# Gathering sampled V rows by two indirect transfers of GpSimd instead of six addressed ones of SP

## The chip, the cores and the metric

The kernel runs on one core of a Trainium2 chip. The metric is the device time of one execution in microseconds; the time before is the median of three runs, 924.11 us (923.51 to 927.22). Times below are us from the start of the profiled execution's span unless ns is said. The engines are PE (TensorE), DVE (VectorE), ACT (ScalarE), POOL (GpSimd) and SP (SyncE), which here only issues transfers.

## The reference

Block-sparse attention over 4 batches, 8 heads, 768 positions and head size 64, followed by a feed-forward layer. Positions are in 24 blocks of 32. A query block sees its neighbours, the first and the last block, and three sampled blocks; the first and last query blocks see all.

```python
mask = np.abs(blk_i - blk_j) <= window
mask = mask | (blk_i == 0) | (blk_j == 0) | (blk_i == n_blocks - 1) | (blk_j == n_blocks - 1)
for qb in range(n_blocks):
    for kb in sampled_blocks[qb]:
        mask[qb*block:(qb+1)*block, kb*block:(kb+1)*block] = True
scores = np.where(mask, scale * q @ k.T, -1e9)
attn = softmax(scores)
x = (attn @ v)            # heads side by side: 3072 tokens x 512
h = x @ w_in              # 512 x 2048
out = np.maximum(0.01 * h, h) @ w_out
```

The sampled block numbers are an input, so which rows are read is known only when the kernel runs.

## The kernel before, in words

Two query blocks of a batch make a tile T (12 a batch; tile 0 holds the first and last block and sees all keys). The other 11 tiles, 44 in all, each get their 12 visible blocks copied together: slots 0 to 3 are the neighbourhood, 4 and 5 the first and last block, 6 to 11 the sampled blocks of the two query blocks. 12 slots of 32 are 384 keys, three chunks of 128.

- `gather_k` fills `kg` from `kt` (K turned, in SBUF): slots 0 to 5 by DVE, the six sampled ones by POOL, as two tasks of three copies (line 1005). Each task first reads three offsets from the small table `offs` into registers (line 982, TENSOR_LOAD).
- `gather_v` fills `vg` from `scr`, a table in DRAM with one row of 2 KB for each position (8 heads, each value split into a high and a low half of 16 bits). Slots 0 to 3 come by one SP transfer of 128 rows, slots 4 and 5 by two SP transfers once a batch and buffer. The six sampled slots are two tasks of SP: a load of three offsets (line 982), then three transfers of 32 rows whose address is a register (line 1036). `vg` has two buffers, so a tile's V can be fetched when PE's products with the tile two before are done.
- A unit is one head pair of a tile. PE makes the scores `s` from `kg` and the turned queries `qs` and `qxs` (heads swapped); DVE adds the mask and takes the maximum (`p`, `mx`); ACT takes the exponential; `pp` is the normalised probability in two halves (ACT the high, DVE the low one); an SP transfer turns it into `pt` (DMA_TRANSPOSE; in the first quarter of the first batch PE does it); PE forms `av` from `pt` and `vg`. ACT and DVE take `av` out as `xf`, and ACT and POOL split it into `x`.
- Four tiles make an item of 256 tokens, whose feed-forward runs beside the attention of later items: PE makes `h` from `x` and the weights `W`, ACT and DVE make `ht`, DVE the high half of `g` and POOL its low half, PE `o`; ACT scales it into `ob` and SP stores it.
- At the start `load_constants` and `build_masks` read the sampled block numbers and build `offs` and the mask; the weights arrive and are decoded until about 250 us.

All of this is recorded as tasks (line 384 is the helper that records most of them), and a planner then sets the order on every engine: it plays the tasks forward with costs from `cost` and `CFG`, each engine taking the ready task of the lowest priority number, and writes down the order. The chip then keeps that order on each engine, with semaphores for what depends on other engines. So a cost in `CFG` or in `cost` is no work; it changes the order. In the order listings `waits PE` means PE's semaphore, `DMAHW` and `DMASW` the counter of an earlier transfer issued by SP or POOL.

Of the kernel before, what the change touches and what calls it, by code (L numbers as in the profile page):

```python
# [16 lines left out]
I32 = mybir.dt.int32  # L17
AF = mybir.ActivationFunctionType
ALU = mybir.AluOpType
AX = mybir.AxisListType  # L20

P = 128
BLOCK = 32
# [5 lines left out]
SLOTS = 12  # L29
# [3 lines left out]
    "ahead": 3,  # L33
    "av_lag": 3,
    "bs": 1500,
    "early": 2,
    "flag": 1,
    "g": 2,
    "g_at": 0,
# [348 lines left out]
def cost(eng, method, a, k):  # L388

    out = k.get("out", a[0] if a else None)  # L390
    n = elements(out)
    apply = lambda x: hasattr(x, "ap")
    if eng == "PE":
        lhs, rhs = a[1], a[2]
        cols = elements(rhs)
        if lhs.dtype == F32:
            return 60.0 + 4 * cols, 300.0 + 4 * cols, "f", []
        half = elements(lhs) <= 64
        t = (cols / 2.4 + 2.5) / CFG["clock"]
        return (t / 2 if half else t), t + 180, ("a" if half else "f"), []  # L400
    if eng == "SP" or method.startswith("dma"):
        turned = method == "dma_start_transpose"
        w = transfer(k["out"], k["in_"], turned)
        rows = len([d for d in list(k["out"].ap) if d[1] > 1])
        busy = 1050.0 + 0.37 * n if turned else 380.0 + 110 * max(0, rows - 1)
        return busy, busy, "", [w]
    if eng == "DVE":
        ptr = sum(1 for x in (k.get("scalar"), k.get("scalar1"), k.get("scale")) if apply(x)) > 0
        src = [x for m, x in k.items() if m in ("in0", "in1", "in_") and apply(x)]
        wide = [x for x in src if elements(x) > 1]  # L410
        f = 1.0
        if method in ("tensor_copy", "tensor_scalar") and len(wide) == 1 and wide[0].space == bass.MemoryType.SB:
            f = 0.5
            if method == "tensor_copy" and wide[0].dtype == F16 and out.dtype == F16:
                f = 0.25
        if method == "tensor_reduce":
            n = elements(k["in_"])
        d = 145 + 62 * ptr + n * f / 0.96
        if len(wide) == 2 and all(x.space == bass.MemoryType.SB for x in wide) and n >= 256:
            d *= 1.08  # L420
        acc = method == "tensor_tensor_reduce"
        return max(d - 70, 60.0), d + 12 + 80 * acc, "", []
    if eng == "ACT":
        src = a[1]
        ptr = any(apply(k.get(x)) for x in ("scale", "bias"))
        d = n * 0.833 + (155 if src.space == bass.MemoryType.PSUM else 187) + 93 * ptr
        acc = "accum_out" in k
        return d - 92 + 100 * acc, d + 14 + 93 * acc, "", []
    d = 120 + n * (2.2 if method == "tensor_tensor" else 1.3)
    return d + 20, d + 12, "", []  # L430
# [3 lines left out]
def tile_block_sparse_attention_ffn(  # L434
# [165 lines left out]
    iota = cst.tile([NB, NB], F32, name="iota")  # L600
    tmps = pf.tile([P, DM], F32, tag="ob", name="tmps", bufs=CFG["ob"])
    sb = tmps[:NB, :2 * NR].bitcast(I32)
    row = tmps[:1, 6:6 + 2 * NB * NR].bitcast(I32)
    eq = tmps[:NB, 150:150 + NR * NB].rearrange("p (r b) -> p r b", r=NR)
    sels = [tmps[:NB, 222 + P * a:222 + P * (a + 1)].rearrange("p (a b c) -> p a b c", a=2, b=2) for a in range(2)]
    assert 222 + 2 * P <= DM and 6 + 2 * NB * NR <= 150
    offs = cst.tile([1, NT - 1, 2, 4], I32, name="offs")
    mask = cst.tile([P, NT - 1, SLOTS], F32, name="mask")

    def load_constants():  # L610
        nc.sync.dma_start(out=eye, in_=c_eye)
        nc.vector.tensor_copy(out=eye16, in_=eye)
        nc.sync.dma_start(out=row, in_=sampled.bitcast(I32).rearrange("(o a) b -> o (a b)", o=1))
        nc.sync.dma_start(out=allow, in_=c_allow)
        nc.sync.dma_start(out=iota, in_=c_iota)
        nc.sync.dma_start(out=sb, in_=sampled.bitcast(I32))

    def build_masks():
        blocks = row.rearrange("p (a b) -> p a b", b=2)[:, NR:NR + (NT - 1) * 2 * NR, 0]
        nc.vector.memset(offs, 0)  # L620
        nc.vector.tensor_scalar(
            out=offs[:, :, :, :NR], in0=blocks.rearrange("p (t a r) -> p t a r", a=2, r=NR), scalar1=0, scalar2=NB - 1,
            op0=ALU.max, op1=ALU.min)
        nc.vector.tensor_scalar(out=offs, in0=offs, scalar1=5, scalar2=None, op0=ALU.logical_shift_left)
        sf = cst.tile([NB, NR], F32, name="sf")
        nc.vector.tensor_copy(out=sf, in_=sb.rearrange("p (a b) -> p a b", b=2)[:, :, 0])

        ok = cst.tile([NB, NR], F32, name="ok")
        hit = cst.tile([NB, NB], F32, name="hit")
        for r in range(NR):  # L630
            nc.vector.tensor_scalar(out=eq[:, r, :], in0=iota, scalar1=sf[:, r:r + 1], scalar2=None, op0=ALU.is_equal)
            nc.vector.tensor_tensor(out=hit, in0=eq[:, r, :], in1=allow, op=ALU.mult)
            nc.vector.tensor_reduce(out=ok[:, r:r + 1], in_=hit, op=ALU.add, axis=AX.X)
            nc.vector.tensor_tensor(out=allow, in0=allow, in1=eq[:, r, :], op=ALU.max)
        nc.vector.tensor_scalar(out=ok, in0=ok, scalar1=-1.0, scalar2=1.0, op0=ALU.mult, op1=ALU.add)

        at = cst.tile([NB, NT - 1, 2, NR], F32, name="at")
        nc.gpsimd.affine_select(
            out=at.rearrange("p t a r -> p (t a) r"), in_=ok.unsqueeze(1).to_broadcast([NB, NB - 2, NR]),
            pattern=[[-1, NB - 2], [0, NR]], base=-1, channel_multiplier=1,  # L640
            compare_op=ALU.is_equal, fill=0.0)
        pm = corner()[:, :(NT - 1) * 2 * NR].rearrange("p (t a r) -> p t a r", t=NT - 1, a=2)
        for a in range(2):
            sel = sels[a]
            nc.vector.memset(sel, 0.0)
            nc.vector.memset(sel[:, :, a, :], 1.0)
            nc.tensor.matmul(
                pm[:, :, a, :], sel.rearrange("p a b c -> p (a b c)"), at[:, :, a, :], start=True, stop=True)
        nc.vector.tensor_scalar(
            out=mask[:, :, 6:], in0=pm.rearrange("p t a r -> p t (a r)"), scalar1=-1.0, scalar2=-NEG,  # L650
            op0=ALU.add, op1=ALU.mult)
        nc.vector.memset(mask[:, :, :6], 0.0)
        for hh in range(2):
            a, b = (slice(D * hh + BLOCK * i, D * hh + BLOCK * (i + 1)) for i in range(2))
            nc.vector.memset(mask[a, :, 3:4], NEG)
            nc.vector.memset(mask[b, :, 0:1], NEG)
            nc.vector.memset(mask[a, 0:1, 4:5], NEG)
            nc.vector.memset(mask[b, NT - 2:NT - 1, 5:6], NEG)
# [318 lines left out]
    kgs, vgs = {}, {}  # L977
    last_use = {}

    def sampled_of(T, a, engine):  # L980

        _, rows = tc.nc.values_load_multi_w_load_instructions(
            offs.ap[:1, T - 1, a, :NR], engines={engine}, min_val=0, max_val=S - BLOCK,
            skip_runtime_bounds_check_because="the block numbers are clamped to the sequence before they are shifted")
        return zip(range(6 + a * NR, 6 + (a + 1) * NR), rows)

    kgb = [pa.tile([P, H, KEYS], F16, tag=f"kg{i}", name=f"kg{i}", bufs=1) for i in range(2)]
    ends = {}
# [1 line left out]
    def gather_k(b, T):  # L990
# [6 lines left out]
        if ends.get(n) != b:  # L997
            ends[n] = b
            nc.vector.tensor_copy(
                out=kg[:, :, P:P + Q2].rearrange("p h (n l) -> p h n l", l=BLOCK),  # L1000
                in_=kt.rearrange("p h (n l) -> p h n l", l=BLOCK)[:, :, 0:NB:NB - 1, :])
        for a in range(2):
            def copies(a=a):
                for slot, off in sampled_of(T, a, mybir.EngineType.Pool):
                    tc.nc.gpsimd.tensor_copy(  # L1005
                        out=kg.ap[:, :, slot * BLOCK:(slot + 1) * BLOCK], in_=kt.ap[:, :, bass.ds(off, BLOCK)])
            at = (6 + a * NR) * BLOCK
            plan.task("POOL", copies, 2150.0, 2150.0, cells(kt) | cells(offs), cells(kg[:, :, at:at + NR * BLOCK]))
            yield
        em = pa.tile([P, KEYS], BF16, tag="em", name=f"em_{b}_{T}", bufs=2)  # L1010
        nc.gpsimd.tensor_copy(
# [8 lines left out]
    def gather_v(b, T):  # L1020
# [6 lines left out]
        if vends.get(n) != b:  # L1027
            vends[n] = b
            for slot, a in ((4, 0), (5, S - BLOCK)):
                ps, c = place(slot)  # L1030
                nc.sync.dma_start(out=vg[ps, c, :], in_=scr[b][a:a + BLOCK, :])
        for a in range(2):
            def moves(a=a):
                for slot, off in sampled_of(T, a, mybir.EngineType.SP):
                    ps, c = place(slot)
                    tc.nc.sync.dma_start(out=vg.ap[ps, c, :], in_=scr[b].ap[bass.ds(off, BLOCK), :])
            into = set()
            for slot in range(6 + a * NR, 6 + (a + 1) * NR):
                ps, c = place(slot)
                into |= cells(vg[ps, c, :])  # L1040
            plan.task("SP", moves, 1850.0, 1850.0, cells(scr[b]) | cells(offs), into, "",
                      [BLOCK * (9.3 + 0.055 * 2048) / 16] * NR)
        vgs[b, T] = vg.rearrange("p c (h x) -> p c h x", h=H)


# [577 lines left out]
```

## Time and profile before

| | |
|---|---|
| Median of the runs | 924.11 us (923.51 to 927.22) |
| Profiled execution | 927.57 us, of it 925.9 us span |
| Busy over the span | PE 83%, DVE 68%, ACT 55%, POOL 36% |
| Transfers issued by SP, all by its hardware queue | 65.7% of the 16 transfer engines' span |
| Sampled V transfers | 264 (44 tiles of six), 88 loads of offsets on SP |
| Sampled K copies | 264 on POOL, 515 ns each in the mean, 88 loads of offsets |

The page gives busy time of each engine and the costliest groups of instructions: count, busy time, mean ns, idle time before them and what ended it. A view by stage gives busy time between two times. The view of waits says which instruction stood idle and which engine or transfer ended that. Of SP the timeline and the view by line show when it issues and how long an issue takes (least, median, most, in ns); SP's issuing does not count as busy time.

### The profile page before, as it was taken

The numbers are of one execution on the slowest core, as the hardware profiler recorded it, in microseconds if no ns is written. First come the engines' busy times: TensorE is split into PE (matmuls) and PEld (weight loads), VectorE is DVE, ScalarE is ACT, GpSimd is POOL, SyncE is SP. The second block draws the span as 40 slices with busy tenths as digits, with TensorE's granted clock in tenths as the row PEclk, the third lists the DMA queues.
The fourth block names the chain that finished last, engine by engine and source line by source line (L and its number), as shares of the span: only waits on it lengthen the run. The fifth ranks groups of instructions, "written<-read, shape, count | busy, mean of one in ns | idle before, by whom it ended". The sixth has DMA issues, their size and how long they took to land. (4 is left out here: it accounts for less than half of the span.)

```text
span 925.9 us, 20826 instructions
## 1 busy us (share of the span) xinstructions
PE 767.3 (83%) x7204; PEld 499.0 (54%) x7204; DVE 626.3 (68%) x1650; ACT 509.4 (55%) x1087; POOL 330.0 (36%) x469
## 2 busy tenths in 40 slices
PE   2647566688889978988788988988898899999998
PEld 2425443444556645555554655655565555656664
DVE  4698789998979945856748657667467466474221
ACT  5678766556655635645546556556357355274121
POOL 0234356523324523433413433324314344242221
PEclk9566678888999999999999999999999999999999
DMA  9504896488797767798677878786765867466000
GB/s 182 201 18 124 256 237 171 115 197 166 149 169 168 169 133 153 155 175 160 138 169 132 169 148 161 177 155 138 166 146 123 161 125 156 89 133 125 1 23 24
DMA packets 312231, 133.29 MB, mean 144 GB/s; under 512 B 275005, under 2 KB 287294, under 8 KB 312126
## 3 DMA queue, kind: packets, MB, share of 16 engines
q1 hardware_dynamic: 312126, 131.96, 65.7%
q8 instruction: 57, 0.93, 0.4%
q14 instruction: 48, 0.39, 0.1%
HBM read 65.57 MB, written 12.58 MB: 84 GB/s over the span
## 5 line engine op out<-in xcount | busy, mean ns | idle before, releaser
L384 PEld LDWEIGHTS <-W 128*128 128x128 f16 (+1 forms) x2480 | 237.8, 101 | 83.6 <-DVE W L384 24.5
L384 PE MATMUL o<-W,g 128*128 128x512 f16 x1152 | 278.1, 388 | 4.0 <-DVE g L384 2.8
L384 PE MATMUL h<-x,W 128*128 128x256 f16 x2304 | 278.4, 276 | 3.0 <-ACT x L384 2.1
L384 POOL TENSOR_TENSOR g<-ht,g 128x512 f16<-128x512 f32 x96 | 117.1, 1220 | 285.0 <-DVE g L384 207.0
L384 PEld LDWEIGHTS <-g 128*128 128x128 f16 x1152 | 109.6, 100 | 132.5 <-issue 21.0
L384 DVE SCALAR_TENSOR_TENSOR pp<-p,r,pp 128x384 f16<-128x384 f32 x208 | 147.6, 738 | 45.6 <-ACT pp L384 45.1
L384 ACT ACTIVATE p<-p,mx 128x384 f32<-128x384 f32 x208 | 125.8, 606 | 91.9 <-DVE mx L384 91.2
L1005 POOL COPY kg<-kt 128x256 f16 x264 | 125.9, 515 | 138.5 <-PE s L384 113.7
L384 ACT ACTIVATE pp<-p,r 128x384 f16<-128x384 f32 x208 | 118.8, 606 | 75.4 <-DMA pt<-pp 26.8
L384 PE MATMUL av<-pt,vg 128*64 128x128 f16 x2112 | 90.5, 228 | 54.5 <-DMA vg<-scr 29.6
L384 DVE SCALAR_TENSOR_TENSOR ht<-h,gd,ht 128x512 f32<-128x512 f32 x80 | 59.9, 749 | 106.3 <-ACT ht L384 105.8
L384 DVE CUSTOM_DVE_ANT_0 p<-s,em,nsc 128x384 f32<-128x384 f32 x176 | 104.7, 609 | 31.6 <-PE s L384 30.6
L384 ACT ACTIVATE ht<-h,gs 128x512 f32<-128x512 f32 x80 | 54.5, 681 | 118.4 <-PE h L384 110.7
L384 PEld LDWEIGHTS <-vg 128*64 128x64 f16 x2112 | 71.8, 114 | 88.4 <-issue 70.2
L384 PE MATMUL s<-kg,qs 128*64 128x384 f16 x352 | 64.0, 354 | 15.9 <-DVE mx L384 14.0
L384 POOL TENSOR_TENSOR x<-xf,x 128x256 f16<-128x256 f32 x48 | 35.9, 747 | 96.2 <-ACT x L384 96.0
L384 PE MATMUL s<-kg,qxs 128*64 128x384 f16 x352 | 63.5, 349 | 4.7 <-DMA qxs<-qs 4.7
L384 PEld LDWEIGHTS <-qs 128*64 128x64 f16 x416 | 29.2, 114 | 40.9 <-issue 32.0
L384 DVE CAST g<-ht 128x512 f16<-128x512 f32 x96 | 42.5, 443 | 10.8 <-PE o L384 6.5
L384 ACT ACTIVATION_READ_ACCUMULATOR p<-p,mx 128x1 f32 x208 | 39.1, 188 | 0.0
L384 DVE TENSOR_SCALAR sum<-sum 128x2 f32<-128x2 f32 x96 | 28.5, 297 | 15.3 <-ACT p L384 14.7
L384 POOL TENSOR_TENSOR W<-W 128x1024 f16<-128x1024 f32 x12 | 28.1, 2349 | 27.9 <-ACT W L384 25.6
(117 smaller groups left out, 759.8 us busy)
## 6 DMA issues: line engine op xcount, KB each, us to landing
vg<-scr SPq DMA_DIRECT2D x280, 64.0 KB, 1.9
vg<-scr SPq DMA_DIRECT2D x44, 256.0 KB, 3.2
v<-in_v_dram SPq DMA_DIRECT2D x32, 192.0 KB, 4.2
qxs<-qs SPq DMA_DIRECT2D x48, 128.0 KB, 2.4
scr<-v SPq DMA_DIRECT2D x16, 384.0 KB, 3.3
rq<-in_q_dram SPq DMA_DIRECT2D x20, 256.0 KB, 3.9
W<-in_moe_w_in_dram SPq DMA_DIRECT2D x5, 1024.0 KB, 7.5
out_dram<-ob SPq DMA_DIRECT2D x20, 256.0 KB, 2.5
```

The lines of the kernel that those rows point to most:

```text
L384: self.plan.task(self.eng, lambda: f(*a, **k), busy, late, reads, writes, kind, loads)
L1005: tc.nc.gpsimd.tensor_copy(out=kg.ap[:, :, slot * BLOCK:(slot + 1) * BLOCK], in_=kt.ap[:, :, bass.ds(off, BLOCK)])
```

## The change

The six sampled transfers of SP and their two loads of offsets go. In their place POOL issues two indirect transfers a tile, which take the row numbers from a table in SBUF, `vrow`, one number for each partition: one fills partitions 64 to 127 of chunk 1 (slots 6 and 7), one the whole of chunk 2 (slots 8 to 11). They come from the same rows of `scr`. `vrow` is built at the start: the block numbers are now copied to all 128 partitions (`rows`), clamped, shifted by 5, and the lane within the block is added (`lane`, by POOL's iota). K's two loads of three offsets become one load of six, whose registers the second task of copies uses too. The planner gets costs for the new tasks, and other costs for an SP transfer (425 instead of 380 ns) and K's copies.

```diff
-    "early": 2,
+    "kcopy": 560.0, "load": 800.0, "fetch": 1100.0, "early": 2,
...
-        busy = 1050.0 + 0.37 * n if turned else 380.0 + 110 * max(0, rows - 1)
+        busy = 1050.0 + 0.37 * n if turned else 425.0 + 110 * max(0, rows - 1)
...
-        nc.sync.dma_start(out=row, in_=sampled.bitcast(I32).rearrange("(o a) b -> o (a b)", o=1))
+        nc.sync.dma_start(
+            out=rows, in_=sampled.bitcast(I32).rearrange("(o a) b -> o (a b)", o=1).to_broadcast([P, 2 * NB * NR]))
...
+        nc.gpsimd.iota(lane.rearrange("p a t -> p (a t)"), pattern=[[0, 2 * (NT - 1)]], base=0, channel_multiplier=1)
+        nc.vector.tensor_scalar(out=lane, in0=lane, scalar1=BLOCK - 1, scalar2=None, op0=ALU.bitwise_and)
+        nc.vector.memset(vrow, 0)
+        for n in range(2 * NR):
+            at, c = (n if n < 2 else n - 2) * BLOCK, int(n >= 2)
+            nc.vector.tensor_scalar(
+                out=vrow[at:at + BLOCK, c, :], in0=of_tile[at:at + BLOCK, :, n], scalar1=0, scalar2=NB - 1,
+                op0=ALU.max, op1=ALU.min)
+        nc.vector.tensor_scalar(out=vrow, in0=vrow, scalar1=5, scalar2=None, op0=ALU.logical_shift_left)
+        nc.vector.tensor_tensor(out=vrow, in0=vrow, in1=lane, op=ALU.add)
...
             def copies(a=a):
-                for slot, off in sampled_of(T, a, mybir.EngineType.Pool):
+                if not a:
+                    found.extend(sampled_of(T, mybir.EngineType.Pool))
+                for slot, off in found[a * NR:(a + 1) * NR]:
...
-        for a in range(2):
-            def moves(a=a):
-                for slot, off in sampled_of(T, a, mybir.EngineType.SP):
-                    ps, c = place(slot)
-                    tc.nc.sync.dma_start(out=vg.ap[ps, c, :], in_=scr[b].ap[bass.ds(off, BLOCK), :])
...
+        for c, n0 in ((1, P - 2 * BLOCK), (2, 0)):
+            at = vrow[:P - n0, c - 1, T - 1:T]
+            into = vg[n0:, c, :]
+
+            def fetch(at=at, into=into):
+                tc.nc.gpsimd.indirect_dma_start(
+                    into.ap, None, scr[b].ap, bass.IndirectOffsetOnAxis(ap=at.ap, axis=0))
+            plan.task("POOL", fetch, CFG["fetch"], CFG["fetch"], cells(scr[b]) | cells(at), cells(into), "",
+                      [(P - n0) * (9.3 + 0.055 * 2048) / 16])
```

The order on SP in the second batch, where its V for one tile is fetched while the next batch's V comes in (`vg0` is the first V buffer, `scr1` the table, `pt4` and `pt5` turned probabilities), before:

```order
L384 DMA_TRANSPOSE pt4_154<-pp0_137 128x6x128 [waits DMAHW0_49,DVE_49,PE_49]
L384 DMA vg0_86<-scr1_72 128x1024 [waits DMAHW1_49,PE_49]
L982 TENSOR_LOAD offs_80
L1036 ISA
L1036 DMA vg0_86<-scr1_72 32x1024 [waits DMAHW2_49,PE_49]
L1036 ISA
L1036 DMA vg0_86<-scr1_72 32x1024 [waits DMAHW3_49]
L1036 ISA
L1036 DMA vg0_86<-scr1_72 32x1024 [waits DMAHW4_49,PE_49]
L384 DMA_TRANSPOSE pt5_155<-pp1_138 128x6x128 [waits DMAHW5_49,DVE_49]
L982 TENSOR_LOAD offs_80
```

And now, at the same tile:

```order
L384 DMA_TRANSPOSE pt2_151<-pp2_144 128x6x128 [waits DMAHW0_49,DVE_49,PE_49]
L384 DMA_TRANSPOSE pt3_152<-pp3_145 128x6x128 [waits DMAHW1_49,DVE_49,PE_49]
L384 DMA v3_110<-in_v_dram 128x6x64 [waits DMAHW2_49]
L384 DMA v3_110<-in_v_dram 128x6x64 [waits DMAHW3_49]
L384 DMA vg0_88<-scr1_72 128x1024 [waits DMAHW4_49,PE_49]
L384 DMA v4_137<-in_v_dram 128x6x64 [waits DMAHW5_49]
L384 DMA v4_137<-in_v_dram 128x6x64 [waits DMAHW6_49]
L384 DMA_TRANSPOSE pt4_156<-pp0_139 128x6x128 [waits DMAHW7_49,DVE_49]
L384 DMA_TRANSPOSE pt5_157<-pp1_140 128x6x128 [waits DMAHW0_49,DVE_49,PE_49]
```

Between the transposes SP has only plain transfers left; the two loads and six moves of the tile are gone.

POOL in the same batch, where one tile's K is copied and the feed-forward goes on (`kg` the K buffers, `g` and `x` the low halves that PE's o and h read), before:

```order
L384 TENSOR_TENSOR g_210<-ht,g_210 128x512 [waits DVE_49]
L982 TENSOR_LOAD offs
L1005 ISA
L1005 COPY kg_85<-kt_83 128x8x32 [waits PE_49]
L1005 ISA
L1005 COPY kg_85<-kt_83 128x8x32
L1005 ISA
L1005 COPY kg_85<-kt_83 128x8x32
L384 TENSOR_TENSOR x_215<-xf,x_215 128x4x64 [waits Activation_49]
L982 TENSOR_LOAD offs
```

And now:

```order
L1055 DMA vg_88<-scr_72,vrow 64x1024 [waits DMASW4_49,PE_49]
L384 TENSOR_TENSOR g_216<-ht,g_216 128x512 [waits DVE_49,Pool_49]
L384 TENSOR_TENSOR x_217<-xf,x_217 128x4x64 [waits Activation_49]
L1055 DMA vg_88<-scr_72,vrow 128x1024 [waits DMASW5_49,PE_49]
L995 TENSOR_LOAD offs
L1021 ISA
L1021 COPY kg_86<-kt_85 128x8x32 [waits PE_49,Pool_49]
```

A fetch that waits for PE now stands ahead of g and x, and another ahead of the next tile's K copies.

DVE in the first 20 us, ahead of the first turned K (`kt`), now (before, the row of `vrow` is not there and the others follow each other in the same way):

```order
L384 CAST eye_76<-eye 128x128
L384 TENSOR_SCALAR vrow<-ob_79 32x11 x5
L384 COPY kt_97<-h_68 128x768
L384 COPY kt_97<-h_67 128x768
L384 TENSOR_SCALAR totk_147<-s_64 128x1
```

Five of the rows that build `vrow` (from the table of block numbers, which lies in an `ob` buffer) stand ahead of K's copies.

More of the change, by code (lines that the diff above doesn't have):

```diff
@@ L602, in tile_block_sparse_attention_ffn @@
     sb = tmps[:NB, :2 * NR].bitcast(I32)
-    row = tmps[:1, 6:6 + 2 * NB * NR].bitcast(I32)
+    rows = tmps[:, 6:6 + 2 * NB * NR].bitcast(I32)
     eq = tmps[:NB, 150:150 + NR * NB].rearrange("p (r b) -> p r b", r=NR)
@@ L606, in tile_block_sparse_attention_ffn @@
     assert 222 + 2 * P <= DM and 6 + 2 * NB * NR <= 150
-    offs = cst.tile([1, NT - 1, 2, 4], I32, name="offs")
+    offs = cst.tile([1, NT - 1, 8], I32, name="offs")
+    vrow = cst.tile([P, 2, NT - 1], I32, name="vrow")
+    lane = cst.tile([P, 2, NT - 1], I32, name="lane")
     mask = cst.tile([P, NT - 1, SLOTS], F32, name="mask")
@@ L618, in build_masks @@
     def build_masks():
-        blocks = row.rearrange("p (a b) -> p a b", b=2)[:, NR:NR + (NT - 1) * 2 * NR, 0]
+        of_tile = rows.rearrange("p (a b) -> p a b", b=2)[:, NR:NR + (NT - 1) * 2 * NR, 0].rearrange(
+            "p (t a) -> p t a", a=2 * NR)
         nc.vector.memset(offs, 0)
         nc.vector.tensor_scalar(
-            out=offs[:, :, :, :NR], in0=blocks.rearrange("p (t a r) -> p t a r", a=2, r=NR), scalar1=0, scalar2=NB - 1,
-            op0=ALU.max, op1=ALU.min)
+            out=offs[:, :, :2 * NR], in0=of_tile[:1], scalar1=0, scalar2=NB - 1, op0=ALU.max, op1=ALU.min)
         nc.vector.tensor_scalar(out=offs, in0=offs, scalar1=5, scalar2=None, op0=ALU.logical_shift_left)
+        nc.gpsimd.iota(lane.rearrange("p a t -> p (a t)"), pattern=[[0, 2 * (NT - 1)]], base=0, channel_multiplier=1)
[8 more added lines that the diff above has]
+        nc.vector.tensor_tensor(out=vrow, in0=vrow, in1=lane, op=ALU.add)
         sf = cst.tile([NB, NR], F32, name="sf")
@@ L978, in tile_block_sparse_attention_ffn, with sampled_of @@
     last_use = {}
-    def sampled_of(T, a, engine):
+    def sampled_of(T, engine):
         _, rows = tc.nc.values_load_multi_w_load_instructions(
-            offs.ap[:1, T - 1, a, :NR], engines={engine}, min_val=0, max_val=S - BLOCK,
+            offs.ap[:1, T - 1, :2 * NR], engines={engine}, min_val=0, max_val=S - BLOCK,
             skip_runtime_bounds_check_because="the block numbers are clamped to the sequence before they are shifted")
-        return zip(range(6 + a * NR, 6 + (a + 1) * NR), rows)
+        return list(zip(range(6, SLOTS), rows))
     kgb = [pa.tile([P, H, KEYS], F16, tag=f"kg{i}", name=f"kg{i}", bufs=1) for i in range(2)]
@@ L1001, in gather_k @@
                 in_=kt.rearrange("p h (n l) -> p h n l", l=BLOCK)[:, :, 0:NB:NB - 1, :])
+        found = []
         for a in range(2):
             def copies(a=a):
-                for slot, off in sampled_of(T, a, mybir.EngineType.Pool):
+                if not a:
+                    found.extend(sampled_of(T, mybir.EngineType.Pool))
+                for slot, off in found[a * NR:(a + 1) * NR]:
                     tc.nc.gpsimd.tensor_copy(
@@ L1007, in gather_k @@
             at = (6 + a * NR) * BLOCK
-            plan.task("POOL", copies, 2150.0, 2150.0, cells(kt) | cells(offs), cells(kg[:, :, at:at + NR * BLOCK]))
+            t = CFG["kcopy"] * NR + (0.0 if a else CFG["load"])
+            plan.task("POOL", copies, t, t, cells(kt) | cells(offs),
+                      cells(kg[:, :, at:at + NR * BLOCK]) | {("registers",)})
             yield
@@ L1031, in gather_v @@
                 nc.sync.dma_start(out=vg[ps, c, :], in_=scr[b][a:a + BLOCK, :])
-        for a in range(2):
-            def moves(a=a):
-                for slot, off in sampled_of(T, a, mybir.EngineType.SP):
-                    ps, c = place(slot)
[L1036 to L1042, printed above, removed]
+        for c, n0 in ((1, P - 2 * BLOCK), (2, 0)):
[6 more added lines that the diff above has]
+                      [(P - n0) * (9.3 + 0.055 * 2048) / 16])
         vgs[b, T] = vg.rearrange("p c (h x) -> p c h x", h=H)
```

## The prediction

> **What bounds the kernel now.** I read the page first (which engine is busy), then busy time by stage, then PE's waits in each stage, because a change to transfers can only pay where PE waits for transfers.
>
> ```profile
> span 925.9 us, 20826 instructions
> PE 767.3 (83%) x7204; PEld 499.0 (54%) x7204; DVE 626.3 (68%) x1650; ACT 509.4 (55%) x1087; POOL 330.0 (36%) x469
> ```
> ```profile
> 0.00:100.00 100.00, 51.26 (x460) 36.33 (x462) 70.86 (x215) 73.19 (x132) 30.00 (x46) 0.71 0.53 141
> 120.00:300.00 180.00, 148.05 (x1336) 94.04 (x1336) 162.31 (x412) 111.33 (x234) 75.50 (x89) 0.90 0.76 171
> 300.00:790.00 490.00, 426.61 (x4193) 273.91 (x4192) 322.40 (x869) 268.17 (x614) 179.72 (x284) 0.99 0.75 153
> 790.00:926.00 136.00, 130.23 (x1091) 85.46 (x1088) 54.24 (x128) 43.98 (x91) 38.85 (x48) 1.00 0.29 64
> ```
>
> Each row gives a stretch, its length, busy time of PE, PE's weight loads, DVE, ACT and POOL, then clock, DMA share and GB/s. There are three regimes. Up to 300 us DVE does most (162.31 of 180 us between 120 and 300). From 300 to 790 us PE is busy 426.61 of 490 us, so 63.4 us are idle. From 790 us on PE runs through the rest of the feed-forward work, 130.23 of 136 us: nothing to win there, and its work does not shrink. So a gain must come out of those 63.4 us, and PE's waits say what they are:
>
> ```profile
> PE av L384 <- DMA vg<-scr: 28.5, 19, 2.7
> PE av L384 <- DMA pt<-pp: 22.7, 25, 2.3
> PE s L384 <- DMA qxs<-qs: 3.6, 3, 1.4
> PE s L384 <- DVE mx L384: 3.5, 4, 2.2
> ```
> ```profile
> PE s L384 <- DVE mx L384: 14.0, 12, 5.1
> PE av L384 <- DMA vg<-scr: 1.1, 1, 1.1
> PE o L384 <- POOL g L384: 1.0, 2, 0.7
> ```
>
> The first fence is 300 to 790 us, the second 120 to 300 us (us in total, times, longest). In the long stage 54.8 of 63.4 us are waits for three kinds of transfer, all issued by SP; before 300 us V costs 1.1 us. SP's own rows show why they are late (first the SP rows of that stage by line, then a stretch of SP and PE in order of time):
>
> ```profile
> L1036 SPq DMA_DIRECT2D vg<-scr x174: 315/316/1650, 316.2 to 785.9; - x174
> L982 SPq TENSOR_LOAD <-offs x58: 664/692/1141, 315.2 to 784.1; - x58
> L982 POOLq TENSOR_LOAD <-offs x55: 726/811/2223, 300.1 to 767.9; - x55
> L384 SPq DMA_TRANSPOSE pt<-pp x131: 1209/1235/3180, 299.4 to 788.9; - x131
> ```
> ```profile
> 546.50 0.49 SPq L384 DMA_DIRECT2D vg<-scr  x1
> 547.97 1.61 SPq L1036 DMA_DIRECT2D vg<-scr  x3
> 549.68 2.58 SPq L384 DMA_TRANSPOSE pt<-pp  x2
> 553.63 1.34 SPq L1036 DMA_DIRECT2D vg<-scr  x3
> 555.02 0.42 SPq L384 DMA_DIRECT2D rq<-in_q_dram  x1
> ```
> ```profile
> 554.53 0.41 PE L384 MATMUL av<-pt,vg 128*64 128x128 f16 x8
> 556.63 0.58 PE L384 MATMUL av<-pt,vg 128*64 128x128 f16 x14 [1.69 <-DMA vg<-scr]
> ```
>
> PE did the first eight matmuls of this group, so the probabilities (pt) were there; then it stood 1.69 us for the second three V blocks, which SP had begun to issue at 553.63, behind two transposes. V alone is late here.
>
> **The change part by part.** *SP loses the sampled moves.* From 546.99 (end of the plain V load) to 549.58 a load of three numbers and three moves took 2.59 us; the second half took from 552.26 to 554.97, 2.71 us. One tile is 5.3 us of SP. 174 moves are 29 tiles in this stage, so 29 x 5.3 = 154 us, or 31% of SP's 490 us, though part of the second half may be waiting. From the medians alone it is 58 x 0.692 + 174 x 0.316 = 95 us, 19%. All of it goes. By itself that is off the path; it counts through the three PE waits.
>
> - V's own wait, 28.5 us: bounds are 0 kept and 28.5 kept. The rows after V come by another queue, and the bytes stay the same (192 rows of 2 KB a tile). I take 70% away, 20 us: the example shows the lateness to be SP's order, and POOL's order (below) will be late in some tiles too.
> - The wait for pt, 22.7 us in 25 times, 0.9 us each: between 0 and all of it is SP's queue. I take 40%, 9 us: a little over the 19 to 31% of SP's time that goes, since a shorter queue waits less than in proportion; the rest is late pp or the transfer itself (2.7 us at the least, next fence).
> - qxs, 3.6 us: half, 2 us.
>
> ```profile
> DMA to landing us min/median/max: 2.7/2.8/5.3
> ```
> ```profile
> vg<-scr SPq DMA_DIRECT2D x280, 64.0 KB, 1.9
> vg<-scr SPq DMA_DIRECT2D x44, 256.0 KB, 3.2
> ```
>
> (The first is pt's; the others are median us from issue to landing.) A fetch of 64 or 128 rows moves 128 or 256 KB and should land in 1.9 to 3.2 us after its issue, if POOL's transfers behave like SP's. That is no later than three separate moves with a load between them.
>
> *POOL gains two fetches a tile.* No row shows an indirect transfer, so I bound its POOL time: below by the plain issue on SP, 0.32 us, above by the longest POOL instruction here, 2.35 us (W, below). I take 1.24 us, near the DMA_TRANSPOSE row, the only issue here that is slower than a plain copy, and near POOL's own g. 58 x 1.24 = 72 us in this stage (19 to 136). One load instead of two gives back about 27 x 0.81 = 22 us. POOL stands at 179.72 busy plus 55 x 0.81 = 45 us of loads, 225 us; it goes to 275 us, 56% of 490 (at the upper end 339 us, 69%). It does not become the bound by sum, but POOL works in order, and a fetch waits until PE has read the buffer (av two tiles earlier). Behind it stand g (for PE's o), x (for h) and kg (for s).
>
> ```profile
> L384 POOL TENSOR_TENSOR g<-ht,g 128x512 f16<-128x512 f32 x96 | 117.1, 1220 | 285.0 <-DVE g L384 207.0 <-DVE r L384 14.6 <-DVE sum L384 13.4
> L384 POOL TENSOR_TENSOR W<-W 128x1024 f16<-128x1024 f32 x12 | 28.1, 2349 | 27.9 <-ACT W L384 25.6 <-issue 2.2
> ```
> ```profile
> POOL g L384 <- DVE g L384: 110.4, 35, 10.2
> POOL kg L1005 <- PE s L384: 81.4, 23, 8.3
> ```
>
> The second fence is 300 to 790 us: POOL stands 110.4 us in 35 times ready before g's input, 3.2 us each, and 81.4 us before kg. Two fetches, 2.5 us, fit into such a gap; where they do not, g is late. Bounds: 0 and 29 x 2.5 = 72 us (every tile's pair straight on the path). PE waited for g only 1.0 us in the rows above, so I take +4 us, near the lower end. If that cover went (fetches of 2.35 us), 4.7 us a tile no longer fits into 3.2 us.
>
> *Contention of DVE and POOL.*
>
> ```profile
> L1005 POOL COPY kg<-kt x264: 387/400/1459, 42.1 to 822.7; 128x256 f16 x132
> L384 DVE SCALAR_TENSOR_TENSOR pp<-p,r,pp x208: 600/617/2475, 36.5 to 852.1; 128x384 f16<-128x384 f32 x104
> L384 DVE SCALAR_TENSOR_TENSOR pp<-p,r,pp 128x384 f16<-128x384 f32 x208 | 147.6, 738 | 45.6 <-ACT pp L384 45.1
> ```
> ```profile
> L1036 SPq DMA_DIRECT2D vg<-scr x42: 315/334/1393, 125.9 to 270.9; - x42
> ```
>
> The two hold each other up already: pp takes 617 ns in the median but 738 in the mean, 208 x 0.121 = 25 us lost beside 330 us of POOL, 0.076 us for each. Where DVE is short (120 to 300 us; the last row: 42 moves start there, 7 tiles) 14 fetches are 17 us of POOL, so pp alone would lose 1.3 us; I take +2 us, between 0 and 17 (DVE held for all of it).
> The Trainium skill, page "SBUF — State Buffer", summary rules for kernel authors, speaks against this change: descriptors of a GpSimd transfer are starved while DVE is in a fast two-port mode, so issue from SP or ACT instead. The rows agree that the engines block each other and do not show it for descriptors. By that page the fetches would be long, and the sum would be that of the slower rival below.
>
> *The start.* DVE gets ten small instructions more; the ones like them take 0.17 us.
>
> ```profile
> L384 DVE TENSOR_SCALAR offs<-ob x1: 173/173/173, 20.3 to 20.3; 1x66 int32<-1x66 int32 x1
> 8.23 0.16 DVE L384 TENSOR_SCALAR totk<-s 128x1 f32<-128x1 f32 x1 [6.11 <-PE s L384]
> 16.69 0.56 DVE L384 COPY kt<-h 128x768 f16<-128x768 f16 x1 [1.53 <-PE h L384]
> ```
>
> lane and the memset of vrow fall into DVE's idle 6.11 us, five vrow rows into the 1.53 us ahead of kt (if the table of block numbers, now 128 copies of 576 bytes, has landed by then; it is asked for at 9 us). Three to four remain, 0.6 us, and the bigger table may be late: +1 us, between 0 and 4.
>
> *The new order everywhere.* The planner's costs move instructions on all engines. PE's idle time in the long stage that is not for transfers is 63.4 - 54.8 = 8.6 us; I take 0, between -9 and +9.
>
> **Sum.** -20 - 9 - 2 + 4 + 2 + 1 = -24 us. The profiled execution took 927.57 us (1.7 outside the span), so 903.6 for that one; it lies 3.5 us above the median of the runs, 924.11, so the median becomes 900.
>
> **The rivals.**
> *The waits change hands.* V is early, but the same SP order leaves pt late, and PE waits for pt instead. For it: 25 waits for pt beside 19 for V, and a pt transfer takes 2.7 us whatever SP does. Against it: in the example pt had landed. Then only a fifth of the 28.5 us stays gained, 6 us, and 2 of qxs, and the new costs of 4 + 2 + 1 us take most: about 923. The Trainium skill, page "DMA: Bandwidth & Descriptors", on issuing engines, agrees with this rival: issuing from several engines saves only the issuer's time, usually small beside the transfer. Here the rows disagree on "small": 19 to 31% of SP.
> *POOL's queue becomes the late one (slower).* A fetch that waits for av, or takes 2.35 us, holds g, and PE's o waits. Place: 300 to 790 us, 29 tiles. For it: POOL waits in order for three other engines already. Against it: the 3.2 us ahead of g. It decides from a fetch of about 2 us: two are then 4 us, over the gap. At 1.5 us of PE a tile, 44 us, less the 31 won: 924 + 13 + 3 = 940.
> *All transfer waits go.* V's, pt's and qxs's 54.8 us, less 7 of new costs: 924 - 48 = 876. For it: all three hang on one queue; against: DMA engines are busy 75% of that stage.
> That the change would not do what it says I rule out for SP: none of the sampled moves and loads is left in its order.
>
> **Chances.** Half a percent, 4.6 us, is about what a measurement of this kernel can tell from no change. Forecast 900: 0.50. Waits change hands: 0.20, of it 0.08 faster and 0.12 within the bound. POOL late: 0.20, slower. All gone: 0.10, faster. So faster 0.68, same 0.12, slower 0.20. The range leaves out half of the two outer cases (0.05 and 0.10): 876 to 936. The likeliest case's own range is 888 to 912: V's wait falls by half or by all (14 to 28 us), with the other terms kept.
>
> **What would show it.** Right: in 300 to 790 us (now a shorter stage) PE's wait for vg under 10 us and for pt around 14; SP without its loads; a fetch on POOL around 1.2 us; PE's wait for g under 6 us. Wrong: fetches over 2 us or stretched beside DVE, a new wait of PE's o or s for POOL's g or kg, a vg wait as long as before with POOL's queue as the issuer, or DVE over 95% busy between 120 and 300 us.

## The result and the profile after

The changed kernel takes 883.27 us in the median (882.06 to 890.77, 4 runs) beside 924.79 us for the kernel before: a ratio of 0.9565, 95% interval 0.9508 to 0.9622. Measured again on another chip it gave 0.9575 (0.9543 to 0.9608); one of those six runs was slow (896.03 us), and the median of the other five is 884.16 us. The forecast was 900 us: the right way and inside the range, but 24 us less where 41.5 us less came, so two fifths too small, and below the likeliest case's own range (888 to 912).

The page of the changed kernel, first the span and the busy time, then its group of pp; the second fence, the fetches, is from the view of POOL's groups:

```profile
span 880.4 us, 19938 instructions
PE 755.9 (86%) x7204; PEld 498.9 (57%) x7204; DVE 625.3 (71%) x1660; ACT 507.5 (58%) x1087; POOL 427.7 (49%) x558
...
L384 DVE SCALAR_TENSOR_TENSOR pp<-p,r,pp 128x384 f16<-128x384 f32 x208 | 141.8, 713 | 24.8 <-ACT pp L384 23.9
```
```profile
L1055 POOL DMA_INDIRECT vg<-scr,vrow x88 | 90.3, 1026 | 52.9 <-PE av L384 29.4 <-issue 10.5 <-PE s L384 6.0
```

Span minus PE's busy time was 158.6 us and is 124.5. Those 34 us are idle time that went; the other 11 are busy time (767.3 to 755.9). The view by stage (length, then PE, weight loads, DVE, ACT, POOL, clock, DMA share, GB/s) shows where; the last stage of 136 us now begins at 745 us:

```profile
120.00:300.00 180.00, 139.22 (x1275) 89.58 (x1274) 162.76 (x402) 107.86 (x223) 87.16 (x99) 0.87 0.78 169
300.00:745.00 445.00, 424.07 (x4287) 278.55 (x4286) 324.14 (x884) 270.35 (x624) 246.30 (x346) 1.00 0.85 171
745.00:881.00 136.00, 127.58 (x1057) 83.39 (x1055) 53.24 (x126) 43.01 (x90) 43.17 (x53) 0.98 0.27 57
```

The long stage has 20.9 us of idle PE in 445, where it had 63.4 in 490: 42.5 us less. Between 120 and 300 us PE does less than before, 139.22 for 148.05 us, so 8.8 us more are idle there. The waits of PE, first from 300 to 745 us, then from 120 to 300 us:

```profile
PE s L384 <- DVE mx L384: 7.0, 6, 1.9
PE av L384 <- DMA pt<-pp: 5.9, 6, 2.5
...
PE s L384 <- DMA qxs<-qs: 0.8, 2, 0.6
PE av L384 <- DMA vg<-scr: 0.7, 1, 0.7
```
```profile
PE s L384 <- DVE mx L384: 22.0, 8, 5.5
PE h L384 <- DVE ht L384: 13.1, 3, 5.6
PE h L384 <- POOL x L384: 2.4, 1, 2.4
...
PE o L384 <- POOL g L384: 1.5, 2, 1.2
```

The three transfers' 54.8 us in the long stage are 7.4. pt went from 22.7 to 5.9, though nothing about pt itself was changed: only SP's queue in front of it and the order. The fetches by line (least, median, most ns of POOL, then the time from issue to landing in us):

```profile
L1055 POOL DMA_INDIRECT vg<-scr,vrow x88: 911/956/1640, 82.5 to 783.0; - x88
...
DMA to landing us min/median/max: 2.9/4.6/9.3
```

### The profile page after: what moved, and what is told of

Read it like the earlier page. It is cut to its first block, busy times and chain, and to the rows that moved or that the text cites. A ratio compares the mean times of both kernels' runs of the same rounds, so it can differ in the third digit from the quotient of the medians.

```text
span 880.4 us, 19938 instructions
## 1 busy us (share of the span) xinstructions
PE 755.9 (86%) x7204; PEld 498.9 (57%) x7204; DVE 625.3 (71%) x1660; ACT 507.5 (58%) x1087; POOL 427.7 (49%) x558
## 5 line engine op out<-in xcount | busy, mean ns | idle before, releaser
L384 PE MATMUL h<-x,W 128*128 128x256 f16 x2304 | 282.7, 279 | 21.4 <-DVE ht L384 13.1
L384 PEld LDWEIGHTS <-W 128*128 128x128 f16 (+1 forms) x2480 | 240.7, 102 | 97.7 <-issue 47.0
L384 PE MATMUL o<-W,g 128*128 128x512 f16 x1152 | 268.4, 380 | 1.5 <-POOL g L384 1.5
L384 PEld LDWEIGHTS <-g 128*128 128x128 f16 x1152 | 107.5, 98 | 128.5 <-issue 14.4
L1021 POOL COPY kg<-kt 128x256 f16 x264 | 132.8, 540 | 66.4 <-PE s L384 41.0
L384 DVE SCALAR_TENSOR_TENSOR pp<-p,r,pp 128x384 f16<-128x384 f32 x208 | 141.8, 713 | 24.8 <-ACT pp L384 23.9
L1055 POOL DMA_INDIRECT vg<-scr,vrow x88 | 90.3, 1026 | 52.9 <-PE av L384 29.4
L384 PE MATMUL av<-pt,vg 128*64 128x128 f16 x2112 | 87.2, 230 | 13.2 <-DMA pt<-pp 6.2
L384 PEld LDWEIGHTS <-vg 128*64 128x64 f16 x2112 | 69.7, 115 | 42.0 <-issue 36.0
L384 DVE SCALAR_TENSOR_TENSOR xf<-av,avt 128x256 f32<-128x256 f32 x48 | 20.1, 419 | 33.9 <-ACT avt L384 33.8
```

The costliest lines, as they stand in the source:

```text
L384: self.plan.task(self.eng, lambda: f(*a, **k), busy, late, reads, writes, kind, loads)
L1021: tc.nc.gpsimd.tensor_copy(out=kg.ap[:, :, slot * BLOCK:(slot + 1) * BLOCK], in_=kt.ap[:, :, bass.ds(off, BLOCK)])
L1055: tc.nc.gpsimd.indirect_dma_start(into.ap, None, scr[b].ap, bass.IndirectOffsetOnAxis(ap=at.ap, axis=0))
```

## The experiments

Three theories stood against each other. *SP*: its time was short, and what left it made all its transfers earlier. *Order*: the planner's new costs did it. *K*: the merged load did it. All ratios are to the kernel before, run beside it.

**1. The planner's costs alone, on the kernel before.**

```diff
-        busy = 1050.0 + 0.37 * n if turned else 380.0 + 110 * max(0, rows - 1)
+        busy = 1050.0 + 0.37 * n if turned else 425.0 + 110 * max(0, rows - 1)
...
-            plan.task("POOL", copies, 2150.0, 2150.0, ...
+            plan.task("POOL", copies, 2480.0, 2480.0, ...
```

> The kernel before with the planner's new costs alone (425 instead of 380 ns for an SP transfer; 2480 instead of 2150 ns for a task of three K copies with their load); no transfer, load or instruction is changed, only the order. Theory SP (the gain is SP's issue time of the sampled V moves and loads that went): 918 to 930 us, ratio to the kernel before 0.993 to 1.006, and PE's waits for vg and pt together still about 50 us. Rival order (the planner's better costs brought the gain): 880 to 900 us and those waits below 25 us.

Measured: 924.75 us, ratio 0.9989 (0.9962 to 1.0017). PE's waits over the whole span nearly stay; first the kernel before, then this run:

```profile
PE av L384 <- DMA vg<-scr: 29.6, 20, 2.7
PE av L384 <- DMA pt<-pp: 25.0, 29, 2.3
```
```profile
PE av L384 <- DMA vg<-scr: 27.1, 21, 2.8
PE av L384 <- DMA pt<-pp: 22.0, 27, 2.0
```

**2. The costs undone, on the changed kernel.**

```diff
-    "kcopy": 560.0, "load": 800.0, "fetch": 1100.0, "early": 2,
+    "kcopy": 716.7, "load": 0.0, "fetch": 1100.0, "early": 2,
...
-        busy = 1050.0 + 0.37 * n if turned else 425.0 + 110 * max(0, rows - 1)
+        busy = 1050.0 + 0.37 * n if turned else 380.0 + 110 * max(0, rows - 1)
```

> The changed kernel with the planner's costs of the kernel before for what both have (380 ns for an SP transfer, 2150 ns for a task of K copies); the fetches keep their cost of 1100 ns. Theory SP: 880 to 892 us. Rival order: over 905 us.

Measured: 886.15 us, ratio 0.9583 (0.9534 to 0.9633), which overlaps the changed kernel's interval. With 1 this rules the costs out as the cause of the gain.

**3. K's merged load alone, on the kernel before.** `gather_k` as changed (one load of six, `offs` as eight numbers a tile, the planner's costs to match); V as before.

```diff
+        found = []
...
-                for slot, off in sampled_of(T, a, mybir.EngineType.Pool):
+                if not a:
+                    found.extend(sampled_all(T, mybir.EngineType.Pool))
+                for slot, off in found[a * NR:(a + 1) * NR]:
```

> The kernel before with K's offsets by one load of six, V still by six SP transfers a tile. Theory SP: 918 to 927 us, PE's waits for vg and pt as before. Rival K: 895 to 910 us.

Measured: 926.75 us, ratio 1.0003 (0.9977 to 1.0029). Nothing.

**4. V's part alone**, K with two loads of three, run twice (the second time beside the changed kernel on the same chip).

```diff
-                if not a:
-                    found.extend(sampled_of(T, mybir.EngineType.Pool))
-                for slot, off in found[a * NR:(a + 1) * NR]:
+                for slot, off in sampled_of(T, a, mybir.EngineType.Pool):
...
-            t = CFG["kcopy"] * NR + (0.0 if a else CFG["load"])
+            t = CFG["kcopy"] * NR + CFG["load"]
```

> The changed kernel with K's two loads of three offsets a tile kept, so V's two fetches are the only thing that differs in kind from the kernel before. Theory SP: 880 to 890 us, since 44 loads of 0.74 us on POOL are off the path. Rival K (the merged load frees POOL for the fetches and carries a good part of the gain): over 895 us.

> V's part of the change alone, K's two loads of three kept: 874 to 880 us, ratio about 0.947 again, if its lead over the changed kernel is real; 880 to 886 us if not.

> The changed kernel once more, beside the one with V's part alone on the same chip. If merging K's loads costs time, it is 5 to 9 us above that one (it was 883.3 against 876.8 us on other chips); if that was the chip or chance, the two agree within 3 us.

Measured: 876.75 us, ratio 0.9472 (0.9424 to 0.9520); again 875.77 us, 0.9481 (0.9458 to 0.9504), beside 884.16 us, 0.9575 (0.9543 to 0.9608), for the changed kernel. V's part carries the whole gain, and the version without the merged load is the faster of the two by 8 us: it beats both kernels. Theory K is wrong even in sign here. By stage (100 to 300 and 300 to 745 us), the changed kernel's second run and then the version with V's part:

```profile
100.00:300.00 200.00, 149.29 (x1412) 98.04 (x1408) 176.50 (x426) 121.89 (x245) 104.59 (x116) 0.85 0.77 165
300.00:745.00 445.00, 422.70 (x4267) 276.61 (x4267) 327.49 (x884) 270.56 (x624) 244.79 (x346) 1.00 0.85 171
```
```profile
100.00:300.00 200.00, 154.09 (x1436) 102.73 (x1433) 179.72 (x427) 121.93 (x246) 102.18 (x114) 0.84 0.74 165
300.00:745.00 445.00, 428.61 (x4323) 279.51 (x4323) 324.41 (x888) 268.92 (x623) 248.68 (x351) 1.00 0.84 172
```

PE gets 4.8 and 5.9 us more done without the merged load. In the first stretch its waits for ht are 8.7 us, where the changed kernel has 12.9; in the second the difference lies in several small waits. Whether the load itself or the order that comes with it costs the 8 us stays open.

**5. SP's old work put back, without V depending on it**: the changed kernel, and SP does two loads and six addressed transfers of 512-byte rows a tile into a scrap buffer.

```diff
+        for a in range(2):
+            def moves(a=a):
+                _, rows = tc.nc.values_load_multi_w_load_instructions(offs.ap[:1, T - 1, a * NR:(a + 1) * NR], ...)
+                for n_, off in enumerate(rows):
+                    tc.nc.sync.dma_start(
+                        out=scrap.ap[n_ * BLOCK:(n_ + 1) * BLOCK, :], in_=scr[b].ap[bass.ds(off, BLOCK), :256])
+            plan.task("SP", moves, 1850.0, 1850.0, ...
```

> The changed kernel, V by POOL's fetches, and in addition SP again does for each tile the two loads of three offsets and six transfers of 32 rows with a register address, 512 bytes a row, into a scrap buffer that nobody reads. So SP has its old issue work, V does not depend on it, and the added bytes are a quarter of V's. If SP's time made the other transfers late (pt, qxs), those waits of PE come back: pt from 7 to 20 us or more, 897 to 912 us. If the gain was only that V itself came earlier: 883 to 890 us and pt's wait stays below 10 us.

Measured: 947.15 us, ratio 1.0240 (1.0190 to 1.0289). V comes by POOL and is in time, and yet the kernel is slower than before:

```profile
PE av L384 <- DMA pt<-pp: 53.4, 43, 4.3
...
PE av L384 <- DMA vg<-scr: 7.5, 6, 2.0
```
```profile
L1062 SPq TENSOR_LOAD <-offs x88: 669/1002/1710, 80.5 to 845.6; - x88
```

So SP's work, not V's path, is what delays the rest: pt's wait is 53.4 us where it is 6.9 over the whole span of the changed kernel. The planner's order changed with the new tasks too, so this run alone does not part the two; 8 does. It went past my 912 us and lies 22 us above the kernel before, with about the same transfer waits in all. Two pieces of that can be read: between 120 and 300 us PE does 137.21 us for 148.05, much as in the changed kernel, and its busy time over the span is 774.1 us for 767.3. Why its busy time rose is not settled.

**6. Only the loads put back on SP.** The edit is that of 5 without the transfers, at a cost of 700 ns.

> The changed kernel with SP's two loads of three offsets a tile put back (registers that nobody uses), no transfers. 88 x 0.69 = 61 us of SP, a third to two fifths of what was taken from it. Theory SP: 885 to 895 us, less than the full burden. If SP has room to spare by now: 880 to 886 us.

Measured: 887.76 us, ratio 0.9577 (0.9534 to 0.9620). The run says nothing on the question: its trace has no load on SP, probably because nobody reads the registers. What is left is the changed kernel in another order, within its interval.

**7. Fixed rows: six transfers on SP, no loads**, on the kernel before. It leaves the sampling of V out: the six transfers read fixed blocks of the table, as many bytes as before, and their addresses are no longer in registers.

```diff
-                for slot, off in sampled_of(T, a, mybir.EngineType.SP):
+                for i_ in range(NR):
+                    slot, off = 6 + a * NR + i_, (T + 3 * a + i_) * BLOCK
...
-                    tc.nc.sync.dma_start(out=vg.ap[ps, c, :], in_=scr[b].ap[bass.ds(off, BLOCK), :])
+                    tc.nc.sync.dma_start(out=vg.ap[ps, c, :], in_=scr[b].ap[off:off + BLOCK, :])
...
-            plan.task("SP", moves, 1850.0, 1850.0, ...
+            plan.task("SP", moves, 1140.0, 1140.0, ...
```

> The kernel before with the six sampled transfers of SP from fixed rows of the table instead of sampled ones, so without the two loads and the register work (it leaves the sampling of V out). SP is rid of 88 x 0.69 us and the register work, not of 264 issues. Theory SP: part of the gain, 895 to 912 us, PE's waits for vg about half. If the number of transfers or their queue is what counts and the loads are nothing: 920 us or more. If the loads are all: 885 us.

Measured: 881.33 us, ratio 0.9515 (0.9475 to 0.9555): as fast as the change, with all 264 transfers still on SP. By line and as one tile stands on SP in order of time:

```profile
L1037 SPq DMA_DIRECT2D vg<-scr x264: 302/419/1932, 82.9 to 792.1; - x132
```
```profile
504.38 0.58 SPq L384 DMA_DIRECT2D vg<-scr  x1
505.01 3.90 SPq L1037 DMA_DIRECT2D vg<-scr  x6
```

The six follow the plain load at once, in 3.9 us; before, they took 5.3 us with a gap of 0.98 and 1.37 us ahead of the threes. The fixed rows do not land sooner: 2.6 us after the issue in the median, 1.9 before.

**8. The same with the planner's old cost**, 1850 ns, so that the planner sees no difference.

> The kernel with fixed rows (six SP transfers a tile, no loads, sampling of V left out), but with the planner's cost of the kernel before (1850 ns for three of them, not 1140), so the planner plans as if the loads were still there. If the loads and the wait for their registers are what SP could not afford: as the kernel with fixed rows, 878 to 892 us. If the lower cost in the planner and the order that follows brought its gain: over 905 us.

Measured: 872.72 us, ratio 0.9429 (0.9399 to 0.9458). In its trace PE, DVE, ACT and POOL carry out the same instructions in the same order as in the kernel before, and SP issues the same transfers in the same order. So 53 us went with the loads and register addresses on SP alone; neither the order nor the planner's cost is the cause. PE's waits over the whole span:

```profile
PE av L384 <- DMA pt<-pp: 6.4, 11, 1.6
PE av L384 <- DMA vg<-scr: 1.2, 1, 1.2
```

**9. One load of six on SP instead of two of three**, on the kernel before; transfers and their register addresses stay. The planner's cost of the tile's second task falls with it (1850 to 1140 ns), so the order changes too.

```diff
+        found = []
...
-                for slot, off in sampled_of(T, a, mybir.EngineType.SP):
+                if not a:
+                    found.extend(sampled_all(T, mybir.EngineType.SP))
+                for slot, off in found[a * NR:(a + 1) * NR]:
```

> The kernel before with one load of six offsets a tile on SP instead of two of three; the six register-addressed transfers stay on SP, K is untouched. It takes 44 of 88 loads away, each about 1 us of SP with the gap around it. If SP's time is short and the loads are its dearest part: about half of what the fixed rows won, 895 to 910 us, and PE's waits for vg and pt about half of 59 us. If two loads less a tile pair change nothing: 918 us or more.

Measured: 905.43 us, ratio 0.9769 (0.9733 to 0.9805): 20 us less with 44 loads fewer and another order. PE's waits over the whole span:

```profile
PE av L384 <- DMA pt<-pp: 20.7, 22, 2.6
PE av L384 <- DMA vg<-scr: 19.7, 14, 4.4
```
```profile
L982 SPq TENSOR_LOAD <-offs x44: 718/736/1771, 83.5 to 822.8; - x44
```

With two, one and no load a tile the kernel takes 925, 905 and 873 to 881 us. The time fell as expected; the waits for vg and pt fell less, to 40 of 55 us.

**10. Four fetches a tile instead of two**, on the changed kernel.

```diff
-        for c, n0 in ((1, P - 2 * BLOCK), (2, 0)):
-            at = vrow[:P - n0, c - 1, T - 1:T]
-            into = vg[n0:, c, :]
+        for i_, (c, n0, m) in enumerate(((1, 64, 32), (1, 96, 32), (2, 0, 64), (2, 64, 64))):
+            at = vrow[:m, i_, T - 1:T]
+            into = vg[n0:n0 + m, c, :]
```

> The changed kernel with four fetches a tile (32, 32, 64 and 64 rows) instead of two (64 and 128): the same rows, 88 POOL instructions more. If a fetch costs POOL about 1 us whatever its rows, POOL gets 80 to 90 us more and stands at some 515 us plus loads. If POOL has room: 880 to 890 us. If POOL's order is the next limit: over 895 us, with PE's waits for POOL's g, x or for vg growing by more than 10 us.

Measured: 886.88 us, ratio 0.9576 (0.9538 to 0.9615), as the changed kernel.

```profile
L1055 POOL DMA_INDIRECT vg<-scr,vrow x176 | 180.9, 1028 | 58.3 <-issue 33.4 <-PE av L384 11.3 <-DMA scr<-v 4.4
```

POOL takes 90 us more in fetches and the time does not move.

## Why the prediction was right, and where it was off

The mechanism was the forecast one: SP's queue made PE wait in the long stage, and taking work from it shortened those waits. In its size the result is nearer to the rival *All transfer waits go*, which I gave 0.10: 47 of the 54.8 us went, and its 876 us is 7 us off, the forecast 17. Of the 45.5 us that the profiled span lost, 42.5 are idle PE time of the long stage and 11.4 PE's busy time, against 8.8 us more of idle time between 120 and 300 us; the rest is under half a microsecond.

- *SP's queue was what the long stage waited for: shown* (7, 8, 9; 5 agrees). Waits of PE for three transfers were to shrink by 31 us and shrank by 47.
- *What counted of SP's relief: only half as I had it.* I charged all of 5.3 us a tile to loads and moves together. Without the loads and the register addresses the six transfers may stay on SP and the kernel is as fast (7, 8). So the transfers' leaving SP was not needed for the gain. Whether it would have been enough by itself, with the loads kept, was not tried: 6 was to show the loads by themselves and had none.
- *V's wait*: -20 us forecast; 28.5 became 0.7 for the plain transfer, and no wait for a fetch is among the rows of that stage, so about -28. Over the whole span PE waited 3.0 us for fetches, three times.
- *pt's wait, the term that was mis-sized*: -9 us forecast by SP's share of time; 22.7 became 5.9, -17. I took the wait to fall by little more than the 19 to 31% of SP's time that went, and it fell by 74%. In 8, with the order of the kernel before, it is 6.4 us over the whole span, where it was 25.0: it is SP's time that did it, not the order.
- *qxs*: -2 forecast, -2.8 measured.
- *A fetch on POOL*: 1.24 us taken, 1.03 in the mean. *Its landing*: 1.9 to 3.2 us forecast, 4.6 in the median, wrong; it was covered, as PE's waits show.
- *POOL's lateness*: +4 us forecast; PE's o waits 1.5 us for g (1.0 before), h 2.4 us for x. The rival that POOL's queue would be late did not come as a wait of PE for g. It shows on ACT: its ht waited 12.7 us for POOL's g between 120 and 300 us, 0.3 before. Fetches themselves waited 29.4 us for PE (the row of POOL's groups), with POOL's later work behind them; four fetches a tile instead of two cost nothing that can be told (10).
- *DVE beside POOL*: +2 us forecast. pp does not show it (738 to 713 ns), and DVE's sum in 120 to 300 us hardly (162.31 to 162.76). One place does. A decode instruction of DVE (W from kt, 128x1024), 1.22 us in the mean before, lasted 5.96 us while POOL worked on x and W; POOL came to these late, behind a fetch that had stood 5.79 us for PE's av. DVE's ht came after the decode, and PE stood 5.63 us for it:

```profile
152.52 0.95 POOL L1055 DMA_INDIRECT vg<-scr,vrow  x1 [5.79 <-PE av L384]
155.57 0.66 POOL L384 TENSOR_TENSOR x<-xf,x 128x256 f16<-128x256 f32 x1
156.20 4.20 POOL L384 TENSOR_TENSOR W<-W 128x1024 f16<-128x1024 f32 x2
```
```profile
155.53 5.96 DVE L384 SCALAR_TENSOR_TENSOR W<-kt,W 128x1024 int32<-128x1024 int32 x1
161.41 0.68 DVE L384 SCALAR_TENSOR_TENSOR ht<-h,ht 128x512 f32<-128x512 f32 x1
```

The second profile of the changed kernel has the same 5.96 us. That POOL held DVE there is my reading of these rows; no run was made to test it. The Trainium skill's rule (page "SBUF — State Buffer", summary rules for kernel authors), that DVE starves such descriptors, does not show in the time on POOL: the longest of 88 fetches held POOL for 1.64 us. Whether it has a part in the late landing, 4.6 us, no run shows.

- *The first 300 us*: +3 us forecast with the start, too little. PE does 8.8 us less between 120 and 300 us, standing 13.1 us for ht, which was no wait there before, and 8 us more for mx. 5.6 of the 13.1 us are the place above; at the other two DVE had other work ahead of ht in its order. The change of order did this, I think; it was not tried. About half of it is gone without the merged load (4).
- *The waits change hands*, which the rule on issuing engines (the Trainium skill, page "DMA: Bandwidth & Descriptors") spoke for: the rows decide against it. The issuer's time was not small here: the loads and register addresses alone were worth 53 us (8).
- *PE's own busy time* fell by 11.4 us, which no term foresaw. It fell as much where V stayed on SP (757.2 us in 7, 756.9 in 8), so it is not POOL's part that did it; its cause is open.

## What to carry to other kernels

Before giving transfers to another engine, look at what stands between them on the issuing queue: here the loads of addresses into registers, two a tile at about a microsecond each with their gap, and the register addresses cost 53 us (8), and without them the six transfers could stay. One load instead of two brought 20 us in a few lines (9). When several unrelated transfers from one queue are late together, look at the queue before the transfers: here pt and qxs, which nobody touched, lost three quarters of their waits in the long stage. To part a cause from the order that a planner makes of it, keep the planner's costs and compare the orders (8); 7 and 8 differ only in a planner's cost, and are 881 and 873 us, on two chips. Run the parts of a change apart: a part that looked like a plain saving (one load for two) made the whole 8 us slower.

## What the runs showed of the hardware

An indirect fetch held POOL for 1.03 us whether it took 32 to 64 rows (1028 ns) or 64 to 128 rows (1026 ns). It landed 4.6 us after its issue in the median, where a plain transfer of 128 rows from SP took 3.2 us before. A load of addresses on SP took 0.69 us in the kernel before, but 1.00 us in the median with SP's work put back (5).
